# Zero products at five early waits of TensorE, and twelve of its products moved behind the loop

## The chip, the core and the metric

The kernel runs on one core of one Trainium2 chip. The metric is the device time of one execution in microseconds (us). A profile is one execution taken with the hardware profiler; its span runs from the first to the last instruction.

## The reference, cut to what matters

The kernel mixes two branches of the same length (2048 tokens, 512 channels) with a gate per token.

```python
g = sigmoid((x * gate_w).sum(-1, keepdims=True))      # x = A_u, 2048 x 512
# branch a: a long convolution, its taps from 128 complex modes per channel
P = exp(logdA[:, :, None] * l[None, None, :])
K = einsum("dn,dnl,dn->dl", Cc, P, dB).real
y = irfft2(rfft2(pad(u)) * rfft2(pad(K)))[..., :L] + u * Dskip
# branch b: a dense layer, F = 1792
h = gelu(x @ w1 + b1)
b = h @ w2 + b2
return g * a + (1 - g) * b
```

## The kernel before, in words

The program has two parts. `front` computes the dense branch, the taps of the convolution and the first stage of its transforms; `conv` does the second stage, the product of the spectra, the way back and the mixing.

**The dense branch in `front`.** The tokens are cut into eight blocks of 256, and the hidden units into two halves of seven columns of 128, so that the loop `dense` has 16 block steps b (eight blocks with the first half of the units, then the same eight with the second half), each cut into four steps j: step number i = 4b + j, 64 in all. Steps j = 0, 1, 2 hold two columns of hidden units, j = 3 holds one. Every float32 operand is split into a high and a low part of type float32r, so one product becomes three. `hidden(i)` does the products with w1 into a PSUM tile `ph` (lines 901 to 903), ScalarE applies the gelu in place (918) and writes the high part `hh` (921), VectorE writes the low part `hl` (931). `output(i)` multiplies these with w2 into the PSUM tiles `acc` (949 to 951), one for each half (s = 0, 1) of the block's tokens; at j = 3 ScalarE scales the sums with 1 - g (970) and a DMA writes them to the output, the second time with an addition. The tiles `hh` and `hl` are two each and taken in turn. The last block's products with w2 (b = 15, steps 60 to 63) are not done in the loop: `output` puts them on the list `late`.

**The taps and the first stage.** The powers of the modes are built on VectorE and ScalarE, 16 chunks of 2 x 64 small products contract them on TensorE (683), and `first_stage` multiplies with the matrix `c1t` (405): eight short products into four PSUM banks, which ScalarE copies out (423 for the signal, 710 for the taps) to be written to DRAM (`tu_d` at 426, `tk_d` at 725). The signal's copies go through two buffers of the tile `attic`, so that a copy can wait for a DMA of two banks before.

**What sets the order in `front`.** Nothing runs when it is written down. Each piece of work is added to a plan with an engine, a duration, a due time and the tiles it reads and writes; a list scheduler then simulates the engines and emits the pieces in the order that results. An engine's program order is fixed by that, and each engine works its list strictly from the top, with semaphores between engines.

**The end.** `conv` is written in its order by hand: 16 steps s, each with two products of the spectra (1113), the pointwise product on VectorE (1135 to 1140), the way back (`inverse`, 1152), and `turn`: ScalarE copies the result out (1158), SyncE stores it to DRAM (1160), and after each eighth part it is loaded back in another layout (1172), into the tiles `den` and `t3`. The dense branch's sums are loaded to SBUF in pairs of token rows (`dense(k)`, 1186: k of the tuple `HERE` on SyncE's queue during the loop, k of `THERE` on ScalarE's queue behind it). `rest(n)` works off n entries of the list `late`, three products each (1197 to 1199): three entries ahead of the last `inverse`, the others behind the loop. Then come four products (1248) that write a PSUM tile `warm` which nobody reads; then VectorE adds the two late sums to the loaded ones (1251); then 32 products bring the convolution back to tokens (`pb`, 1259), which VectorE (1271) or ScalarE and GpSimd (1268, 1269) scale, add and store (1275, 1273).

Ahead of the first product of `front` stand 13 products of a zero tile `dm` with itself (1010).

Of the kernel before, what the change touches and what calls it, by code (L numbers as in the profile page):

```python
# [9 lines left out]
F32 = mybir.dt.float32  # L10
F32R = mybir.dt.float32r
I32 = mybir.dt.int32
AF = mybir.ActivationFunctionType
ALU = mybir.AluOpType
# [3 lines left out]
P = 128  # L18
L = 2048
D = 512  # L20
# [3 lines left out]
FH = NF // 2  # L24
H = 2
DH = D // H
SB = 256
# [40 lines left out]
D_OUT = -5.37  # L68
N_LATE = 2
N_REST = 3  # L70
N_KEEP = 4

N_ATTIC, N_LOFT, N_TK = 11, 8, 8
ASIDE = (1, 3, 6, 8, 11, 13)
HERE, THERE = (7, 0, 1, 2, 3, 4), (5, 6)
N_DEN = 8
# [200 lines left out]
def gated_mix(  # L277
# [41 lines left out]
    def front(pool, psum, keep, attic, loft, den):  # L319
# [54 lines left out]
        )  # L374
        hh, hl = (tiles(N_HL, [P, 2, SB], n, F32R, keep) for n in ("hh", "hl"))

        io = tiles(2, [P, D], "io")
        gs = pool.tile([P, 16], F32, name="gs")
        dm = pool.tile([P, P], F32, name="dm")
        b2r = pool.tile([P, D], F32R, name="b2r")  # L380
        ones = pool.tile([P, P], F32R, name="ones")
# [11 lines left out]

        def first_stage(xs, due, evac, ahead=2):

            q = (step[0] + ahead) % N_H
            banks = [(phs[q].rearrange("p a b -> p (a b)"), ("h", q)), (pks[0].rearrange("p g s -> p (g s)"), ("pk", 0))]
            banks += [(pus[k], ("pu", k)) for k in range(2)]

            def products():  # L400

                for r, (bank, _) in enumerate(banks):
                    rs = slice(32 * r, 32 * r + 32)
                    for m, (x, _) in enumerate(xs):
                        nc.tensor.matmul(bank[64 * m : 64 * m + 64], c1t[rs], x[rs], start=True, stop=True)  # L405

            mm(1.2, products, due + D_S1, [*(key for _, key in xs), "c1"], [key for _, key in banks], 0.5)
            for r, (bank, key) in enumerate(banks):
                evac(r, bank, key)
# [3 lines left out]
        def signal():  # L413
            for s in range(8):
# [14 lines left out]

                first_stage(xs, t, evac)  # L430
            yield None
# [449 lines left out]
        def halves(i):  # L881

            n = len(cols(i))
            if i in (4 * NB - 4, 4 * NB - 3):
                j = i % 4
                js = slice(2 * j, 2 * j + n)
                return xh[0][:, js], xlo[0][:, js], ("xh", 0, j), ("xl", 0, j)
            k = i % N_HL
            return hh[k][:, 0:n], hl[k][:, 0:n], ("hh", k), ("hl", k)

        def hidden(i, t):
# [4 lines left out]
            def products(n, f):  # L896
                w = f % FH
                for d in range(4):
                    ds = slice(d * P, (d + 1) * P)
# [35 lines left out]
        def output(i, t):  # L935
# [4 lines left out]
            def products(s, a):  # L940
                ss = slice(s * P, (s + 1) * P)
                start = j == 0
                if start and b < NSB:
                    nc.tensor.matmul(a, ones, b2r, start=True, stop=False)
                    start = False
# [9 lines left out]
            for s in range(2):  # L955
                if b == NB - 1 and s >= 2 - N_LATE:
                    for n, f in enumerate(fs):
                        late.append((s, hi[:, n], lo[:, n], wh[1][f % FH], wl[1][f % FH]))
                    continue
# [115 lines left out]
    def conv(pool, ps, late, attic, loft, den):  # L1075
# [112 lines left out]
        def rest(n):  # L1188

            while late and n:  # L1190
# [3 lines left out]
                if first:  # L1194
                    accs[s] = ps.tile([P, D], F32, tag=f"pk{s}", name=f"acc{s}", bufs=1)
                ss = slice(s * P, (s + 1) * P)
                nc.tensor.matmul(accs[s], h[:, ss], w, start=first, stop=False)
# [44 lines left out]
        for k in THERE:  # L1242
            dense(k, nc.scalar)
        rest(14)

        warm = ps.tile([P, D], F32, tag="pa0", name="warm", bufs=1)
        for _ in range(N_KEEP):
            nc.tensor.matmul(warm[0:64], mats[7][1][:, 1], zs[0], start=True, stop=True)
        for s in range(N_LATE):
            z = mos[7][:, s]  # L1250
            nc.vector.scalar_tensor_tensor(z, accs[s], gate[:, 1, 14 + s : 15 + s], z, ALU.mult, ALU.add)

# [103 lines left out]
```

## Time and profile before

| | |
|---|---|
| three timed runs | 532.12, 534.57 and 536.15 us, median 534.57 us |
| the profiled execution | 529.8 us |
| its span | 528.0 us |
| TensorE busy | 509.9 us, 97% of the span |
| VectorE, ScalarE, GpSimd busy | 426.8, 353.5, 41.4 us |
| mean granted TensorE clock | 0.988 |
| DMA | 107.87 MB, mean 204 GB/s |

A busy time counts an instruction from its start to its modelled end; products overlap, so that the distance from start to start is what one costs in a row. "idle before <- releaser" in a row says how long the engine stood still ahead of the instruction, and whose end let it go. PE is TensorE, PEld its loading of weights, DVE VectorE, ACT ScalarE, POOL GpSimd, SP SyncE; a q behind the name is the engine's queue of DMA issues.

### The profile page before, as it was taken

The page shows a single profiled execution, that of the slowest core. Times are in us where ns is not written, and L with a number is a line of the kernel's source. Part 1 is how long each engine was busy: PE and PEld are TensorE (multiplying, and loading weights), DVE is VectorE, ACT ScalarE, POOL GpSimd, SP SyncE. Part 2 cuts the span into 40 slices and gives each one's busy share as a digit, 9 for nine tenths or more (in the row PEclk, how much of TensorE's full clock was granted, in tenths as well). Part 3 has the DMA queues.
Part 4 walks back from the last instruction along what each step waited for, and adds up shares of the span by engine and source line. Part 5 has one row for each costly group of instructions (what it writes and reads, how often), then busy time and mean ns, then how long its engine had stood idle before and what let it go on. Part 6 is the DMA issues. An engine that isn't in the chain of part 4 may idle for free.

```text
span 528.0 us, 12214 instructions
## 1 busy us (share of the span) xinstructions
PE 509.9 (97%) x4818; PEld 386.5 (73%) x4818; DVE 426.8 (81%) x806; ACT 353.5 (67%) x614; POOL 41.4 (8%) x79
## 2 busy tenths in 40 slices
PE   8869999999999999999999999999999999999995
PEld 7537789898889988986998998988889832222441
DVE  5899899999999969879999999999801177777523
ACT  4989946699875599986686998366533545565312
POOL 2000000000000000000112011102010100110113
PEclk9969999999999999999999999999999999999999
DMA  7998674162585434393979027715678988999987
GB/s 248 361 302 300 206 247 137 57 202 61 149 211 216 150 85 129 110 313 84 227 168 269 2 81 134 162 28 121 200 206 171 242 278 303 362 332 397 350 286 287
DMA packets 82517, 107.87 MB, mean 204 GB/s; under 512 B 39334, under 2 KB 43562, under 8 KB 81916
## 3 DMA queue, kind: packets, MB, share of 16 engines
q1 hardware_dynamic: 76476, 85.04, 50.8%
q0 software_dynamic: 5056, 18.65, 13.8%
q10 hardware_dynamic: 928, 3.41, 1.8%
q8 instruction: 38, 0.62, 0.5%
q14 instruction: 19, 0.16, 0.1%
HBM read 61.46 MB, written 45.62 MB: 203 GB/s over the span
## 4 chain that ended last, share of the span: by engine, by line
PE 78%; ACT 10%; DMA 8%; DVE 1%; issue 1%; SPq 1%; ACTq 0%; DVEq 0%
PE pk L683 10%; PE ph L901 8%; PE acc L949 8%; PE ph L903 8%; PE ph L902 8%; PE acc L951 7%; PE acc L950 7%; PE p2u L1113 6%; PE p2k L1113 5%; DMA tu_d<-attic 3%; PE pa L1152 3%; PE pb L1259 3%; PE ph L405 2%; ACT ph L918 2%; ACT L918 1%
## 5 line engine op out<-in xcount | busy, mean ns | idle before, releaser
L901 PE MATMUL ph<-xh,wh 128*128 128x256 f32 x448 | 129.3, 289 | 3.8 <-ACT attic L423 2.2
L903 PE MATMUL ph<-xh,wl 128*128 128x256 f32 x448 | 127.9, 285 | 0.4 <-DVE wl L784 0.2
L902 PE MATMUL ph<-xlo,wh 128*128 128x256 f32 x448 | 127.6, 285 | 0.0
L901 PEld LDWEIGHTS ph<-xh,wh 128*128 128x128 f32 x448 | 86.3, 193 | 14.2 <-issue 5.6
L902 PEld LDWEIGHTS ph<-xlo,wh 128*128 128x128 f32 x448 | 86.4, 193 | 2.0
L903 PEld LDWEIGHTS ph<-xh,wl 128*128 128x128 f32 x448 | 86.2, 192 | 1.0 <-DVE wl L784 1.0
L949 PE MATMUL acc<-wh,hh 128*128 128x512 f32 x210 | 84.6, 403 | 2.4 <-ACT hh L921 2.4
L951 PE MATMUL acc<-wh,hl 128*128 128x512 f32 x210 | 82.5, 393 | 0.0
L950 PE MATMUL acc<-wl,hh 128*128 128x512 f32 x210 | 82.4, 393 | 0.0
L918 ACT ACTIVATE ph<-ph,b1t 128x256 f32<-128x256 f32 x112 | 50.4, 450 | 43.5 <-PE ph L903 41.5
L931 DVE TENSOR_TENSOR hl<-ph,hh 128x512 fp32r<-128x512 f32 (+1 forms) x62 | 38.3, 618 | 30.6 <-ACT hh L921 30.3
L683 PE MATMUL pk<-y,den 128*32 128x64 f32 x2048 | 61.4, 290 | 0.0
L683 PEld LDWEIGHTS pk<-y,den 128*32 128x32 f32 x2048 | 57.2, 136 | 3.7 <-issue 1.4
L949 PEld LDWEIGHTS acc<-wh,hh 128*128 128x128 f32 x210 | 39.5, 188 | 17.1 <-issue 6.8
L951 PEld LDWEIGHTS acc<-wh,hl 128*128 128x128 f32 x210 | 39.4, 188 | 10.0 <-DVE hl L931 1.3
L645 DVE TENSOR_TENSOR y<-y,ea 128x64 f32<-128x64 f32 (+4 forms) x80 | 45.3, 566 | 0.2
L950 PEld LDWEIGHTS acc<-wl,hh 128*128 128x128 f32 x210 | 39.5, 188 | 6.6
L921 ACT CAST hh<-ph 128x512 fp32r<-128x512 f32 (+1 forms) x62 | 33.0, 532 | 10.3 <-PE acc L950 6.9
L490 DVE TENSOR_TENSOR loft<-den,zz 128x256 f32<-128x256 f32 (+2 forms) x48 | 37.3, 776 | 1.8 <-ACT den L616 1.4
L491 DVE TENSOR_TENSOR loft<-den,zz 128x256 f32<-128x256 f32 (+2 forms) x48 | 37.2, 774 | 0.0
L658 DVE TENSOR_TENSOR y<-y,loft 128x2048 f32<-128x2048 f32 x16 | 36.5, 2284 | 0.0
L1121 ACT COPY k<-p2k 128x512 f32<-128x512 f32 x32 | 18.7, 585 | 24.9 <-issue 13.1
(180 smaller groups left out, 876.5 us busy)
## 6 DMA issues: line engine op xcount, KB each, us to landing
tu_d<-attic SPq DMA_DIRECT2D x64, 128.0 KB, 3.4
tk_d<-sk SPq DMA_DIRECT2D x32, 256.0 KB, 5.1
t_d<-sa SPq DMA_DIRECT2D x32, 256.0 KB, 5.5
tk<-tk_d SPq DMA_DIRECT2D x24, 256.0 KB, 3.8
t<-t_d POOLq DMA_DIRECT2D x9, 512.0 KB, 6.9
attic<-in_xt_dram SPq DMA_DIRECT2D x16, 256.0 KB, 4.1
xh_d<-xh SPq DMA_DIRECT2D x8, 512.0 KB, 3.9
xl_d<-xlo SPq DMA_DIRECT2D x8, 512.0 KB, 3.8
```

The costliest lines, as they stand in the source:

```text
L490: vec(2 * m, lambda: vv.tensor_mul(t, a, br), due, [ka, *kb], [kt])
L645: nc.vector.tensor_mul(both(n, 64 - 3 * n, n), both(0, 64 - n, n), an)
L683: nc.tensor.matmul(pks[q][32 * j : 32 * j + 32, :, gg], x[:, r, :, ch], y[:, r, :, ch], start=(r == 0), stop=(r == 1), skip_group_check=True,)
L901: nc.tensor.matmul(p, h, xh[xk][:, d], start=(d == 0), stop=False)
L902: nc.tensor.matmul(p, h, xlo[xk][:, d], start=False, stop=False)
L903: nc.tensor.matmul(p, lo, xh[xk][:, d], start=False, stop=(d == 3))
L918: nc.scalar.activation(phs[q][:, n], phs[q][:, n], AF.Gelu_apprx_tanh, bias=b1t[:, f : f + 1])
L931: nc.vector.tensor_sub(lo, phs[q][:, 0:nf], hi.bitcast(F32))
L949: nc.tensor.matmul(a, h, wh[1][w], start=start, stop=False)
L950: nc.tensor.matmul(a, h, wl[1][w], start=False, stop=False)
L951: nc.tensor.matmul(a, l, wh[1][w], start=False, stop=(j == 3))
L1113: nc.tensor.matmul(out[64 * i : 64 * i + 64], w, x, start=True, stop=True)
```

## The change

Three things change in TensorE's list, and what follows from them elsewhere.

1. A tile `nil` of 128 x 128 zeros is made by GpSimd at the very start, and a helper `busy(n)` multiplies it with itself n times (float32, two passes each). It is called at five places of `front`: 4 times within step 1 ahead of its second column, 5 times ahead of the first output product (step 0), 6 and 4 times in the second `first_stage` of the signal (ahead of its first bank and ahead of its third), and 5 times ahead of step 2's hidden products: 24 products. Where `busy` names no bank, it adds its zeros to the sum in `acc[0]`.
2. The output products of step 58 (b = 14, j = 2: two columns, two token halves, three products each, so twelve) leave the loop and join `late`; they sum up in two more PSUM tiles, in banks `pu2` and `pu3`. For that, `hh` and `hl` get a third tile, which step 58 alone uses. `rest` behind the loop does up to 18 entries where it did up to 14, and VectorE adds four late sums where it added two (0.75 us each in the profile before).
3. The four products into `warm` are gone.

With them the order of the loads changes: the sums of tokens' pair 6 are loaded during the loop (second in `HERE`), and pairs 4 and 5 instead of 5 and 6 behind it. Lines of the changed kernel stand 10 to 16 lower.

```diff
-HERE, THERE = (7, 0, 1, 2, 3, 4), (5, 6)
+HERE, THERE = (7, 6, 0, 1, 2, 3), (4, 5)
-N_LATE = 2
-N_KEEP = 4
+FILL_H, FILL_O, FILL_U = (4, 5), 5, (6, 4)
-        hh, hl = (tiles(N_HL, [P, 2, SB], n, F32R, keep) for n in ("hh", "hl"))
+        hh, hl = (tiles(N_HL + 1, [P, 2, SB], n, F32R, keep) for n in ("hh", "hl"))
+        nil = pool.tile([P, P], F32, name="nil")
+        nc.gpsimd.memset(nil, 0.0)
+
+        def busy(n, bank=None):
+            to = acc[0][:, 0:P] if bank is None else bank[:, 0:P]
+            for _ in range(n):
+                nc.tensor.matmul(to, nil, nil, start=bank is not None, stop=bank is not None)
...
+                busy(fill[0])
                 for r, (bank, _) in enumerate(banks):
+                    if r == 2:
+                        busy(fill[1])
...
-                first_stage(xs, t, evac)
+                first_stage(xs, t, evac, fill=FILL_U if s == 1 else (0, 0))
...
-            k = i % N_HL
+            k = N_HL if i == 4 * NB - 6 else i % N_HL
...
+                if (i, n) == (1, 1):
+                    busy(FILL_H[0], phs[q][:, n])
+                elif (i, n) == (2, 0):
+                    busy(FILL_H[1])
...
+                if (i, s) == (0, 0):
+                    busy(FILL_O, a)
...
-                if b == NB - 1 and s >= 2 - N_LATE:
+                if b == NB - 1 or i == 4 * NB - 6:
                     for n, f in enumerate(fs):
-                        late.append((s, hi[:, n], lo[:, n], wh[1][f % FH], wl[1][f % FH]))
+                        late.append((s + 2 * (NB - 1 - b), hi[:, n], lo[:, n], wh[1][f % FH], wl[1][f % FH]))
...
-                    accs[s] = ps.tile([P, D], F32, tag=f"pk{s}", name=f"acc{s}", bufs=1)
-                ss = slice(s * P, (s + 1) * P)
+                    accs[s] = ps.tile([P, D], F32, tag=f"pu{s}" if s > 1 else f"pk{s}", name=f"acc{s}", bufs=1)
+                ss = slice(s % 2 * P, s % 2 * P + P)
...
-        rest(14)
-
-        warm = ps.tile([P, D], F32, tag="pa0", name="warm", bufs=1)
-        for _ in range(N_KEEP):
-            nc.tensor.matmul(warm[0:64], mats[7][1][:, 1], zs[0], start=True, stop=True)
-        for s in range(N_LATE):
-            z = mos[7][:, s]
-            nc.vector.scalar_tensor_tensor(z, accs[s], gate[:, 1, 14 + s : 15 + s], z, ALU.mult, ALU.add)
+        rest(18)
+
+        for s in range(4):
+            m, i = 7 - s // 2, s % 2
+            z, g = mos[m][:, i], gate[:, 1, 2 * m + i : 2 * m + i + 1]
+            nc.vector.scalar_tensor_tensor(z, accs[s], g, z, ALU.mult, ALU.add)
```

TensorE's order near the end of the loop, before: the last six of step 58's twelve output products (those into `acc1` with `hh0`), the six of step 59 (`hh1`), and the first hidden products of step 61.

```order
L950 MATMUL acc1_86<-wl14_135,hh0_138 128x512
L951 MATMUL acc1_86<-wh14_121,hl0_140 128x512
L949 MATMUL acc1_86<-wh15_122,hh0_138 128x512
L950 MATMUL acc1_86<-wl15_136,hh0_138 128x512
L951 MATMUL acc1_86<-wh15_122,hl0_140 128x512
L949 MATMUL acc0_85<-wh16_123,hh1_139 128x512
L950 MATMUL acc0_85<-wl16_137,hh1_139 128x512
L951 MATMUL acc0_85<-wh16_123,hl1_141 128x512
L949 MATMUL acc1_86<-wh16_123,hh1_139 128x512
L950 MATMUL acc1_86<-wl16_137,hh1_139 128x512
L951 MATMUL acc1_86<-wh16_123,hl1_141 128x512
L901 MATMUL ph1_88<-xh10_107,wh02_112 128x256
```

The same place in the changed kernel, from the last hidden product of step 60 on.

```order
L917 MATMUL ph0_87<-xh10_107,wl01_125 128x256
L965 MATMUL acc0_85<-wh16_123,hh1_139 128x512
L966 MATMUL acc0_85<-wl16_137,hh1_139 128x512
L967 MATMUL acc0_85<-wh16_123,hl1_142 128x512
L965 MATMUL acc1_86<-wh16_123,hh1_139 128x512
L966 MATMUL acc1_86<-wl16_137,hh1_139 128x512
L967 MATMUL acc1_86<-wh16_123,hl1_142 128x512
L915 MATMUL ph1_88<-xh10_107,wh02_112 128x256
```

All twelve products of step 58 are gone from here; step 59's now follow step 60's hidden products directly. Nothing else in the order of this place has moved.

They stand again behind the loop, as `acc2` and `acc3` with the third tile `hh2`; here the last of the six rows with `acc2`, the six with `acc3` and the first of the final products `pb`, in the changed kernel.

```order
L1215 MATMUL acc2_5517<-wh15_122,hl2_143 128x512
L1213 MATMUL acc3_5524<-wh14_121,hh2_140 128x512
L1214 MATMUL acc3_5524<-wl14_135,hh2_140 128x512
L1215 MATMUL acc3_5524<-wh14_121,hl2_143 128x512
L1213 MATMUL acc3_5524<-wh15_122,hh2_140 128x512
L1214 MATMUL acc3_5524<-wl15_136,hh2_140 128x512
L1215 MATMUL acc3_5524<-wh15_122,hl2_143 128x512
L1273 MATMUL pb00_5535<-den_78,g1t_4807 64x512 x2
L1273 MATMUL pb01_5536<-den_78,g1t_4807 64x512 x2
```

The twelve products have taken the place of the four into `warm`, which stood directly ahead of `pb00`.

The third place is early in TensorE's list: the second first stage of the signal and the start of step 2, in the changed kernel, with the semaphores that each row waits for.

```order
L386 MATMUL acc_85<-nil 128x128 x6
L415 MATMUL ph_89<-attic,c1t 64x512 [waits DMAHW2_49,Activation_49]
L415 MATMUL ph_89<-ux_103,c1t 64x512 [waits DMAHW3_49]
L415 MATMUL pk_90<-attic,c1t 64x512 [waits Activation_49]
L415 MATMUL pk_90<-ux_103,c1t 64x512
L386 MATMUL acc_85<-nil 128x128 x4
L415 MATMUL pu_91<-attic,c1t 64x512 [waits Activation_49]
L415 MATMUL pu_91<-ux_103,c1t 64x512
L415 MATMUL pu_92<-attic,c1t 64x512 [waits Activation_49]
L415 MATMUL pu_92<-ux_103,c1t 64x512
L386 MATMUL acc_85<-nil 128x128 x5
L915 MATMUL ph_89<-xh_106,wh_114 128x256 [waits Activation_49]
```

The three rows with `nil` are added; they wait for nothing, and each stands directly ahead of a row that waits. The rows around them are those of before, in the same order. ScalarE's list is the same as before throughout, and the planner's order of all other work too.

2 lines of the change are left out of this document (1 added, 1 removed).

## The prediction

> **What bounds the kernel now.** I read the page's first part and its shares of the chain of work that ended last.
>
> ```profile
> PE 509.9 (97%) x4818; PEld 386.5 (73%) x4818; DVE 426.8 (81%) x806; ACT 353.5 (67%) x614; POOL 41.4 (8%) x79
> PE 78%; ACT 10%; DMA 8%; DVE 1%; issue 1%; SPq 1%; ACTq 0%; DVEq 0%
> ```
>
> TensorE (PE) is busy for 97% of the span and makes 78% of the chain. The 8% of DMA must lie somewhere too. Busy time by stage, with instruction counts and the granted clock, separates the stages:
>
> ```profile
> 26.40:30.00 3.60, 1.56 (x6) 0.53 (x4) 3.42 (x12) 3.58 (x8) 0.00 (x0) 1.00 0.91 260
> 30.00:33.00 3.00, 1.80 (x13) 0.51 (x14) 2.96 (x8) 2.99 (x5) 0.00 (x0) 0.63 0.97 278
> 36.00:39.60 3.60, 3.54 (x16) 3.55 (x17) 3.60 (x6) 2.16 (x4) 0.00 (x0) 0.50 1.05 376
> 39.60:43.00 3.40, 3.40 (x26) 1.96 (x24) 2.98 (x8) 3.34 (x7) 0.00 (x0) 0.80 0.78 221
> 60.00:100.00 40.00, 40.00 (x474) 33.85 (x473) 39.28 (x73) 26.53 (x46) 0.25 (x2) 1.00 0.46 152
> 240.00:395.00 155.00, 155.00 (x1862) 135.59 (x1860) 138.25 (x247) 103.00 (x169) 17.71 (x31) 1.00 0.55 139
> 460.00:490.00 30.00, 30.00 (x157) 8.18 (x152) 24.34 (x40) 16.61 (x32) 3.75 (x8) 1.00 1.00 367
> ```
>
> The columns are the stretch, its length, then PE, PEld, DVE, ACT, POOL, the clock, the DMA share and GB/s. From 60 us on PE hardly rests: a product removed there is time gained. Before, it rests, and from about 31 to 41 us it has lost its clock: 0.63, 0.50, 0.80 in the three stretches. Whether that costs anything depends on who is late there, which the chain in order of time tells:
>
> ```profile
> 33.65 0.45 SPq L426
> 34.16 3.68 DMA tu_d<-attic
> 37.91 0.59 ACT attic L423
> 48.32 5.01 DMA tu_d<-attic
> 57.48 0.60 ACT io L970
> 58.13 0.50 PE acc L944
> ```
>
> The chain runs through the signal's stores to `tu_d`, the copies on ScalarE that wait for their two buffers (423), ScalarE's other work, and reaches PE only at 58.13. PE's own waits in this stretch are in its timeline:
>
> ```profile
> 13.49 0.39 PE L901 MATMUL ph<-xh,wh 128*128 128x256 f32 x1 [1.59 <-DVE wh L780]
> 17.87 0.50 PE L949 MATMUL acc<-wh,hh 128*128 128x512 f32 x1 [1.97 <-ACT hh L921]
> 29.26 1.04 PE L405 MATMUL ph<-attic,c1t 32*64 32x512 f32 x2 [2.04 <-DMA attic<-in_xl_dram]
> 32.56 1.11 PE L405 MATMUL pu<-attic,c1t 32*64 32x512 f32 x1 [1.20 <-ACT attic L423]
> 36.05 0.58 PE L901 MATMUL ph<-xh,wh 128*128 128x256 f32 x1 [1.52 <-ACT attic L423]
> 47.10 0.39 PE L901 MATMUL ph<-xh,wh 128*128 128x256 f32 x1 [0.72 <-ACT attic L423]
> 58.13 0.50 PE L944 MATMUL acc<-b2r,ones 128*128 128x512 f32 x1 [0.90 <-ACT io L970]
> ```
>
> The first five are the five places of the change. The last two matter most: after the cold stretch PE still arrives early, twice, and stands for ScalarE.
>
> **Part 1: the zero products.** They add 24 products of 128 columns in two passes. The nearest row is that of the products ahead of the first step, 26 passes of the same shape:
>
> ```profile
> 1.00 5.92 PE L1010 MATMUL pk<-dm 128*128 128x128 f32 x26 [1.00 <-POOL dm L1005]
> 0.74 0.20 POOL L1005 MEMSET dm<- 128x128 f32 x1 [0.29 <-POOLq L1337]
> ```
>
> 5.92 / 13 = 0.455 us a product is the upper end. The lower end takes a quarter of the 0.43 us that a pass of 512 columns into `warm` costs (shown below): 0.107 a pass, 0.215 a product. So the five fills cost 0.86 to 1.82, 1.08 to 2.28, 1.29 to 2.73, 0.86 to 1.82 and 1.08 to 2.28 us against waits of 1.59, 1.97, 2.04, 1.20 and 1.52. At the lower end all lie inside their waits. At the upper end they overrun by 0.23 + 0.31 + 0.69 + 0.62 + 0.76 = 2.61 us, of which the waits at 47.10 and 58.13 take 0.72 + 0.90 = 1.62, so that about 1.0 us would reach the path. I take zero: the clock was full ahead of the first three fills. Behind the fills stand, on PE's list, first-stage products that ScalarE copies out, and step 2's hidden products, whose gelu ScalarE only reaches behind its own queue, so a small overrun makes nobody late.
>
> What can the fills win? If they hold the clock, step 2's 24 hidden products, which begin at 36.05, run faster. The stretch from 36 to 39.6 has 17 of their weight loads in 3.60 us, 0.21 each; at full clock it is
>
> ```profile
> 45.86 0.28 PE L901 MATMUL ph<-xh,wh 128*128 128x256 f32 x1
> 45.98 0.28 PE L902 MATMUL ph<-xlo,wh 128*128 128x256 f32 x1
> ```
>
> 0.12 from start to start: 24 x 0.09 = 2.2 us. But what follows is the row at 47.10, where PE already waits 0.72 us for a copy on ScalarE, and ScalarE hangs on the DMAs of the chain, not on PE. The 2.2 us turn into a longer wait at 47.10 and at 58.13. I take zero of it, and keep 2.2 as the other end.
>
> The new `memset` on GpSimd comes ahead of the `memset` of `dm` and shifts GpSimd's start by its 0.20 us. PE's first products follow, but the wait of 1.59 at 13.49 swallows that; of SyncE's first loads some may shift by up to 0.2 us. I take 0.1.
>
> **Part 2: twelve products leave the loop.** The first and the thirteenth of the last 18 output products in the loop:
>
> ```profile
> 409.13 0.39 PE L949 MATMUL acc<-wh,hh 128*128 128x512 f32 x1
> 411.88 0.39 PE L949 MATMUL acc<-wh,hh 128*128 128x512 f32 x1
> ```
>
> The twelve before the thirteenth are step 58's: 411.88 - 409.13 = 2.75 us. PE is full there, so whatever follows comes 2.75 us sooner, provided its inputs do. Step 59's six products need `hh` and `hl` of their step, ready long enough by VectorE's row:
>
> ```profile
> 405.99 0.42 DVE L931 TENSOR_TENSOR hl<-ph,hh 128x256 fp32r<-128x256 f32 x1 [2.62 <-ACT hh L921]
> ```
>
> It ends at 406.41, against 409.13. Between loop and second stage, PE waits for the last gelu and a copy, both behind PE's own last hidden product, so they shift along.
>
> **Part 3: behind the loop.** Here the twelve products add 2.75 us again, and `warm` goes:
>
> ```profile
> 505.11 3.15 PE warm L1248 x7
> 508.69 13.77 PE pb L1259 x61
> 505.52 0.14 PEld L1248 LDWEIGHTS warm<-z,cc 128*64 128x64 f32 x1 [0.29 <-issue]
> 507.67 0.14 PEld L1248 LDWEIGHTS warm<-z,cc 128*64 128x64 f32 x1 [0.29 <-issue]
> ```
>
> `warm` is four products of two passes; their weight loads, the second and the seventh shown, follow each other at (507.67 - 505.52) / 5 = 0.43 us, so eight passes hold PE for 3.44 us. The chain goes from `rest` through it into `pb` without a gap. If `pb` may start as soon as `rest` ends, the end moves by -2.75 + 2.75 - 3.44 = **-3.44 us**. What would be late next are the DMAs that `pb` reads, which have so far been hidden behind `rest` and `warm`. Their issues, the time to landing of the first of each, and PE's first use of `t3`:
>
> ```profile
> 502.75 1.16 ACTq L1172 DMA_DIRECT2D den<-t_d  x2
> 504.01 1.84 ACTq L1172 DMA_DIRECT2D t<-t_d  x3
> den<-t_d ACTq DMA_DIRECT2D x1, 256.0 KB, 3.0
> t<-t_d ACTq DMA_DIRECT2D x1, 512.0 KB, 5.8
> 511.11 0.19 PEld L1259 LDWEIGHTS pb<-t,g1t 128*64 128x64 f32 x2
> ```
>
> `den` lands at 502.75 + 3.0 = 505.75 and the first of `t3` at 504.01 + 5.8 = 509.81. Both follow the last `inverse`, so they move to 503.0 and 507.06. PE then wants `den` at about 505.1 and `t3` at 511.11 - 3.44 = 507.67: margins of 2.1 and 0.6 us. The second is thin, and the DMAs are full in the second stage (a share of 1.00 in 460 to 490), so they may not come the whole 2.75 us sooner. If they came no sooner at all, `t3` would hold `pb` to 509.81, which is 1.30 us sooner than the 511.11 of before instead of 3.44. I take 0.1 us for this, with both ends kept.
>
> VectorE's two further additions take 0.75 us each; the last starts when `rest` ends and is over at about 505.9, ahead of the first `pb` sum, which comes at 509.60 - 3.44 = 506.16 by this row:
>
> ```profile
> 509.60 0.75 DVE L1271 SCALAR_TENSOR_TENSOR attic<-pb,gate,attic 128x512 f32<-128x512 f32 x1 [3.70 <-PE pb L1259]
> ```
>
> The bank of `acc3` is wanted by the fourth `pb` sum, later still. The token pair 6, which these additions need, is loaded during the loop, tens of us ahead.
>
> **The sum.** 0 (fills) + 0.1 (start) - 2.75 + 2.75 - 3.44 + 0.1 (landing) = -3.24, so about 3.2 us off: the profiled execution would go from 529.8 to 526.6 us. The three runs lie 2.3 to 6.4 us above the profiled one; taking the same off their median gives 534.57 - 3.2 = **531.4 us**, 0.6% less. A measurement of this kernel can tell about 1% from no change.
>
> **The rivals.**
> *The DMAs hold the end.* They stay where they are, the gain is the 1.30 us above: 533.3 us. For it speaks the full share, against it that from 423 to 429 us the share is far lower, so there is room to start sooner.
>
> ```profile
> 427.00:429.00 2.00, 2.00 (x12) 0.68 (x10) 2.00 (x4) 1.40 (x3) 0.00 (x0) 1.00 0.49 119
> ```
>
> *The early clock is worth its time.* In executions without the profiler, PE may be colder for longer and reach 58 us last; then the fills save the 2.2 us above: 534.57 - 3.2 - 2.2 = 529.2. The spread of the three runs, 4 us, allows it; the waits at 47.10 and 58.13 speak against it.
>
> *Slower: the end runs at half clock.* Without `warm`, PE may stand ahead of `pb` or of `t3`. The early stretch shows what follows from thin work: after waits of 2.04 and 1.20 us with first-stage products between, the clock went to 0.50, for about 10 us (31 to 41). If the same befell `pb`, its products, one pair of passes in 0.43 us, would take double: 10 us at half pace lose 5 us, with the wait of 2 us that starts it 7; against 3.44 gained that is 3.6 slower: 538.1 us. It decides from a wait of some 2 us on, that is if the DMAs land 1.4 us or more later than the margin allows. The Trainium skill, "TensorE: Matmul & The Clock Gate", section "HAM oscillation — how this bites in real kernels", gives as the rule that only idle gaps of PE above about 3.4 us bring the clock down; by it a wait of 2 us would cost nothing but itself, and the time would be 531.4 + 2 = 533.4. The trace does not bear it out: no gap from 26.4 to 36.05 us exceeds 2.04, and the clock still halved; so this rival keeps a small chance.
>
> *The change doesn't do what it says:* the fills start too late or run half-clocked, and their 1.0 us comes on top: 531.4 + 1.0 = 532.4, inside my range.
>
> **How the numbers follow.** Forecast 55% (alone 530.0 to 533.0), DMAs 15%, early clock 17%, half clock at the end 7%, the rest 6%, spread (fills that cost are among it). The range takes in the first three with the runs' own spread around them: 526.5 to 535.5 us. Faster by over 1% means below 529.2: about half of the early-clock case and some luck of the runs, 0.18. Slower by over 1% means above 539.9: the worse part of the half-clock case and the unexplained, 0.08. Within 1%: 0.74.
>
> **What would show it.** In the changed profile: zero products inside all five early waits, a clock of 1.00 in 30 to 41 us, and longer waits at the two rows now at 47.10 and 58.13, the latter's start unmoved; the second stage 2.75 us sooner; `pb` directly behind `rest`, at about 505, with at most 0.5 us of waiting for `t3`. Wrong would be a start at 58 that moved by over 1 us, a wait of PE in the second stage, or a clock below 1.00 at the end.

## The result, and the profile after

In the session with the first measurement the changed kernel took 528.67 us (median of six runs, 526.88 to 530.85) against 535.21 us for the kernel before (six runs, 531.36 to 536.15). The ratio is 0.990, with a 95% interval of 0.9862 to 0.9938: 5.3 us less, between 3.3 and 7.4. (It is not the quotient of the two medians, which lie 6.5 us apart.) Measured again in a later session it was 0.9916 (0.9884 to 0.9948), 4.5 us less. The forecast was 531.4 us, 3.2 us less, inside 526.5 to 535.5.

The profiled execution took 528.3 us with a span of 526.5 (before 529.8 and 528.0). The first part of the page after, and its shares of the chain:

```profile
PE 509.1 (97%) x4858; PEld 387.8 (74%) x4858; DVE 428.4 (81%) x808; ACT 353.0 (67%) x614; POOL 41.6 (8%) x80
PE 75%; ACT 11%; DMA 8%; DVE 3%; issue 2%; SPq 1%; ACTq 0%; DVEq 0%
```

Forty more instructions on TensorE and about the same busy time: 48 zero passes came, eight warming ones went. Busy time by stage, with the granted clock as the third number from the end, in the stretches that were cold before:

```profile
30.00:33.00 3.00, 3.00 (x20) 1.35 (x16) 2.76 (x9) 2.99 (x5) 0.00 (x0) 1.00 0.91 232
36.00:39.60 3.60, 3.49 (x30) 3.19 (x36) 3.60 (x4) 1.91 (x4) 0.00 (x0) 1.00 0.98 340
39.60:43.00 3.40, 1.45 (x14) 0.30 (x14) 2.33 (x7) 3.34 (x7) 0.00 (x0) 1.00 0.59 157
43.00:46.00 3.00, 3.00 (x24) 2.45 (x21) 2.46 (x10) 2.93 (x5) 0.00 (x0) 1.00 1.04 351
```

The clock is full throughout (0.63, 0.50 and 0.80 before). TensorE's timeline shows the five fills and the waits of TensorE from there to 60 us:

```profile
12.12 1.05 PE L386 MATMUL ph<-nil 128*128 128x128 f32 x8
15.19 1.28 PE L386 MATMUL acc<-nil 128*128 128x128 f32 x10
17.91 0.50 PE L965 MATMUL acc<-wh,hh 128*128 128x512 f32 x1 [1.21 <-ACT hh L935]
26.77 1.50 PE L386 MATMUL acc<-nil 128*128 128x128 f32 x12
28.91 1.04 PE L415 MATMUL ph<-attic,c1t 32*64 32x512 f32 x2 [0.64 <-DMA attic<-in_xl_dram]
30.49 1.16 PE L386 MATMUL acc<-nil 128*128 128x128 f32 x8
33.62 1.38 PE L386 MATMUL acc<-nil 128*128 128x128 f32 x10
36.11 0.39 PE L915 MATMUL ph<-xh,wh 128*128 128x256 f32 x1 [1.11 <-ACT attic L433]
42.55 0.64 PE L415 MATMUL pu<-attic,c1t 32*64 32x512 f32 x1 [1.95 <-ACT attic L433]
47.41 0.38 PE L915 MATMUL ph<-xh,wh 128*128 128x256 f32 x1 [0.72 <-ACT attic L433]
58.32 0.50 PE L960 MATMUL acc<-b2r,ones 128*128 128x512 f32 x1 [0.79 <-ACT io L986]
```

A fill of 12 passes takes 1.50 us, 0.125 a pass. Behind three of the fills a wait is left (1.21, 0.64 and 1.11 us); the products behind the first and the fourth, at 13.16 and 31.58 us, wait no longer and start sooner than before (13.49 and 32.56). What TensorE gained between 36 and 43 us it hands back in a new wait of 1.95 us at 42.55, and it starts at 58.32, where it started at 58.13. The end of the chain:

```profile
495.77 0.60 ACT sa L1174
...
496.51 6.42 DMA t_d<-sa
...
503.02 2.87 DMA den<-t_d
...
506.02 13.97 PE pb L1273 x64
...
520.02 0.75 DVE attic L1285
```

`pb` begins 2.67 us sooner than before (508.69), and in this execution it waits for `den`: the last store to `t_d` took 6.42 us. VectorE's last operation ends 2.46 us sooner. The end of the span moved by only 1.5 us because what follows that operation took 5.7 us (526.5 - 520.77) instead of 4.8 (528.0 - 523.23); in the other profiles below it takes 4.7 to 7.4, whatever the kernel.

### The profile page after: what moved, and what is told of

It reads as the page before. It is cut to its first block, busy times and chain, and to the rows that moved or that the text cites. A ratio compares the mean times of both kernels' runs of the same rounds, so it can differ in the third digit from the quotient of the medians.

```text
span 526.5 us, 12296 instructions
## 1 busy us (share of the span) xinstructions
PE 509.1 (97%) x4858; PEld 387.8 (74%) x4858; DVE 428.4 (81%) x808; ACT 353.0 (67%) x614; POOL 41.6 (8%) x80
## 4 chain that ended last, share of the span: by engine, by line
PE 75%; ACT 11%; DMA 8%; DVE 3%; issue 2%; SPq 1%; ACTq 0%; DVEq 0%
PE pk L693 10%; PE ph L915 8%; PE ph L917 8%; PE ph L916 8%; PE acc L965 8%; PE acc L967 7%; PE acc L966 7%; PE p2u L1129 6%; PE p2k L1129 5%; PE pa L1168 3%; PE pb L1273 3%; DMA tu_d<-attic 2%; PE ph L415 2%; ACT L932 2%; ACT ph L932 2%
## 5 line engine op out<-in xcount | busy, mean ns | idle before, releaser
L915 PEld LDWEIGHTS ph<-xh,wh 128*128 128x128 f32 x448 | 85.1, 190 | 11.9 <-issue 5.6
L916 PEld LDWEIGHTS ph<-xlo,wh 128*128 128x128 f32 x448 | 85.2, 190 | 2.0
L917 PEld LDWEIGHTS ph<-xh,wl 128*128 128x128 f32 x448 | 85.1, 190 | 1.2 <-DVE wl L794 1.2
L965 PE MATMUL acc<-wh,hh 128*128 128x512 f32 x206 | 82.9, 403 | 1.3 <-ACT hh L935 1.2
L967 PE MATMUL acc<-wh,hl 128*128 128x512 f32 x206 | 81.1, 394 | 0.4 <-DVE hl L945 0.4
L966 PE MATMUL acc<-wl,hh 128*128 128x512 f32 x206 | 80.9, 393 | 0.0
```

Of the source, the lines that this page charges most:

```text
L915: nc.tensor.matmul(p, h, xh[xk][:, d], start=(d == 0), stop=False)
L916: nc.tensor.matmul(p, h, xlo[xk][:, d], start=False, stop=False)
L917: nc.tensor.matmul(p, lo, xh[xk][:, d], start=False, stop=(d == 3))
L965: nc.tensor.matmul(a, h, wh[1][w], start=start, stop=False)
L966: nc.tensor.matmul(a, h, wl[1][w], start=False, stop=False)
L967: nc.tensor.matmul(a, l, wh[1][w], start=False, stop=(j == 3))
```

## The experiments

All ratios are against runs of the kernel before in the same session; the sessions of the experiments ran on three different chips. This table has from each profile the starts, in us, of the first tap product (683 before, 693 after), of the second stage (1113, 1129), and of `pb`, with TensorE's wait for `den` ahead of it.

| kernel | first tap product | second stage | `pb` | wait |
|---|---|---|---|---|
| before | 65.97 | 420.53 | 508.69 | 0 |
| changed | 66.18 | 418.29 | 506.02 | 0.42 |
| fills alone | 67.56 | 422.75 | 510.92 | 0 |
| move alone | 67.23 | 419.93 | 507.25 | 0 |
| no `warm` | 67.49 | 423.03 | 509.37 | 1.74 |
| changed with `warm` | 67.92 | 421.31 | 512.21 | 0 |
| more fills | 65.87 | 420.62 | 507.94 | 0 |
| double fills | 66.47 | 420.37 | 507.68 | 0 |
| changed again | 66.92 | 419.02 | 506.33 | 0 |
| stores split | 67.97 | 420.32 | 507.62 | 0 |
| stores split, more fills | 66.16 | 419.85 | 507.15 | 0 |
| more fills again | 67.13 | 420.64 | 509.06 | 1.11 |
| eight elsewhere | 66.15 | 418.63 | 505.94 | 0 |
| third stage and sixteen | 67.90 | 420.62 | 507.93 | 0 |

Two things are to be read from it first. The first column differs by 1.5 us between kernels with the same program up to that point (before and no `warm`), and by 1.7 among the changed kernel, its repeat and the one with `warm`: a single profile cannot size the fills. And from the second stage to `pb` it is 87.30 to 87.32 us in every kernel with the move and without `warm` in which `den` was in time, against 88.16 before: that part is TensorE's program alone.

### The two halves of the change

The fills alone: the kernel before with the 24 zero products; the twelve products stay in the loop and `warm` stays behind it.

```diff
+        nil = pool.tile([P, P], F32, name="nil")
+        nc.gpsimd.memset(nil, 0.0)
...
+                busy(fill[0])
...
+                if (i, s) == (0, 0):
+                    busy(FILL_O, a)
```

> The kernel before plus the 24 zero products and nothing else. Theory A (the early stretch hangs on ScalarE and the DMAs, PE only waits): clock 1.00 in 30 to 41 us, the start at 58 us unmoved, time within 1 us of before. Theory B (in the timed runs PE is colder than in the profiled one and is late at 58 us): the mean clock of the runs goes from about 0.98 to 0.99 or more, and the median falls by 3 to 5 us, most of the change's 6.5.

532.12 us, ratio 0.9981 (0.9962 to 1.0): 1.0 us less, between 2.0 and nothing. Busy time and clock by stage in the profile of this kernel:

```profile
43.00:46.00 3.00, 2.46 (x6) 0.85 (x7) 2.46 (x10) 2.95 (x4) 0.00 (x0) 0.50 1.08 367
46.00:49.00 3.00, 3.00 (x16) 3.00 (x15) 3.00 (x6) 2.92 (x7) 0.00 (x0) 0.50 0.94 305
```

The row of TensorE's timeline that begins the cold stretch:

```profile
43.54 1.11 PE L415 MATMUL pu<-attic,c1t 32*64 32x512 f32 x1 [1.94 <-ACT attic L433]
```

The cold spell has not gone but moved: the wait that the faster TensorE now has in the third first stage of the signal, 1.94 us with thin products around it, takes the clock to 0.50 from 43 to 49 us. In the profile of the changed kernel the same wait (1.95 us) did not. The time fell as the first theory allows (1 us at most); 3 to 5 us, as the second has it, lie outside the interval, though the mean clock of the runs did rise, from 0.985 to 0.99 in the median.

In its new place the cold spell is not free. The chain of work that ended last, in this profile:

```profile
43.00 0.50 ACT attic L433
43.54 1.97 PE pu L415 x4
45.51 0.51 PE ph L915
```

From 43.54 on the chain stays on TensorE up to the first tap product: TensorE waits for ScalarE neither near 47 nor near 58 us, since it now comes too late there itself. From the product at 43.54 to the first tap product it is 24.02 us here. Five profiles of this study have a wait at the same product and a full clock behind it (changed, move alone, no `warm`, stores split with more fills, third stage and sixteen): there it is 23.0 to 23.6 us, of which 0.9 to 1.5 are waits and 22.1 are work. So the cold clock cost TensorE 1.9 us, of which the waits took up the larger part and 0.4 to 1.0 us were paid.

The move alone: the changed kernel with all fills at nothing and without `nil`.

```diff
-FILL_H, FILL_O, FILL_U = (4, 5), 5, (6, 4)
+FILL_H, FILL_O, FILL_U = (0, 0), 0, (0, 0)
...
-        nil = pool.tile([P, P], F32, name="nil")
-        nc.gpsimd.memset(nil, 0.0)
+        nil = None
```

> The changed kernel without its zero products. Theory A: 3.2 us faster than before if TensorE sets the end, 1.3 to 1.5 us if the DMAs behind the last store to t_d hold it. Theory B: the same 1.3 to 1.5 us; the mean clock of the runs stays at the level of before.

528.52 us, ratio 0.9929 (0.9897 to 0.996): 3.8 us less, between 2.1 and 5.5. The clock is at half early on, as before (0.50 from 33 to 39.6 us), and the end of the chain has no wait:

```profile
507.02 0.23 PE acc L1214
507.25 13.91 PE pb L1272 x64
521.18 0.75 DVE attic L1284
```

What the move is worth can be read more closely than from the times. The start of the last chunk of tap products, of the second stage, and of VectorE's last operation, in the kernel before:

```profile
382.82 3.84 PE L683 MATMUL pk<-y,den 128*32 128x64 f32 x128
420.53 1.08 PE L1113 MATMUL p2k<-tk,cc 128*64 128x512 f32 x4
522.48 0.75 DVE attic L1271
```

The first two in this kernel; the third stands in the chain above:

```profile
384.95 3.84 PE L692 MATMUL pk<-y,den 128*32 128x64 f32 x128
419.93 1.08 PE L1128 MATMUL p2k<-tk,cc 128*64 128x512 f32 x4
```

From the last chunk to the second stage it is 37.71 us before and 34.98 here: 2.73 less. From there to VectorE's last operation it is 101.95 and 101.25: 0.70 less. Both repeat within 0.02 us in the other profiles, the first in all kernels with the move (34.98 or 34.99) and all without (37.70 or 37.71), the second wherever the loads at the end were in time.

So the move is worth what the sum gave it, and the fills about 1 us more. The two ratios multiply to 0.991, which is the whole change.

### What `warm` hid

The kernel before without `warm`, the twelve products still in the loop:

```diff
-        warm = ps.tile([P, D], F32, tag="pa0", name="warm", bufs=1)
-        for _ in range(N_KEEP):
-            nc.tensor.matmul(warm[0:64], mats[7][1][:, 1], zs[0], start=True, stop=True)
```

> The kernel before without the four products into warm, whose result nobody reads. If TensorE sets the end: 3.4 us faster, pb at 505.2. If the DMAs hold it: den lands at about 505.8, so pb waits 0.6 us or so for it and the end comes 1.5 to 2.5 us sooner; the moved products would then add little. If the wait costs the clock: pb at half clock, 3 to 6 us slower.

532.08 us, ratio 0.9975 (0.9948 to 1.0003): 1.3 us less, where the products that went had held TensorE for 3.44. TensorE's timeline tells where the rest is:

```profile
509.37 3.65 PE L1256 MATMUL pb<-den,g1t 128*64 128x512 f32 x16 [1.74 <-DMA den<-t_d]
```

And the busy time by stage, with the clock, around and behind this wait:

```profile
508.00:510.00 2.00, 0.63 (x4) 0.40 (x6) 0.42 (x1) 0.00 (x0) 0.00 (x0) 1.00 0.89 307
510.00:515.00 5.00, 4.85 (x25) 1.69 (x22) 2.21 (x3) 1.38 (x2) 2.38 (x2) 1.00 0.92 347
```

Without the twelve products behind the loop, `rest` ends before `den` is there. `warm` covered that landing; in the changed kernel the moved products do. Behind this wait comes a shorter one for the first load of `t3` (`t` in the rows), which the chain goes through:

```profile
507.51 5.52 DMA t<-t_d
513.17 10.54 PE pb L1256 x48
```

The stretch from the second stage to VectorE's last operation is 100.70 us here, 1.25 shorter than before (101.95): of the 3.44, 1.74 went in the wait for `den` and 0.45 in the one for `t3`. That agrees with the 1.3 us of the timed runs. And after 1.74 us of standing still the clock stayed at 1.00.

The changed kernel with the four products of `warm` put back behind `rest`:

```diff
         rest(18)
+        warm = ps.tile([P, D], F32, tag="pa0", name="warm", bufs=1)
+        for _ in range(4):
+            nc.tensor.matmul(warm[0:64], mats[7][1][:, 1], zs[0], start=True, stop=True)
```

> The changed kernel with the four products into warm put back behind the late products. TensorE then starts pb as late as before (about 508.5 us). If TensorE sets the end, this costs the 3.4 us again and leaves only what the zero products bring; if the DMAs hold the end, it costs less than 3.4, 1 to 2 us. Against before: Theory A 0 to 1 us faster, Theory B 3 to 5 us faster.

531.2 us, ratio 0.9965 (0.9942 to 0.9988), 1.9 us less than before and so 2.6 more than the changed kernel's 0.9916. In the chain they stand where they stood:

```profile
508.63 3.15 PE warm L1264 x7
511.84 0.37 PE warm L1264
512.21 13.76 PE pb L1277 x61
```

From 508.63 to 512.21 it is 3.58 us. With the move done TensorE pays for all of `warm`: from the second stage to VectorE's last operation it is 104.69 us, 3.44 more than the 101.25 without it. The difference of the ratios, 2.6 us, is between two sessions and has an uncertainty of some 2; 1.9 us less than before lies between what the two theories gave.

### Filling the moved cold spell

Three and five zero products more, in the third first stage of the signal:

```diff
+                    if r == 3 and len(fill) > 2:
+                        busy(fill[2])
...
-                first_stage(xs, t, evac, fill=FILL_U if s == 1 else (0, 0))
+                first_stage(xs, t, evac, fill=FILL_U if s == 1 else (3, 0, 5) if s == 2 else (0, 0))
```

> The changed kernel plus eight zero products in the signal's third first stage: three ahead of its first bank and five ahead of its fourth, where two profiles with zero products showed a wait of TensorE of up to 1.95 us at 42 us and, behind it, half clock from 43 to 52 us. Theory C (the zero products move the cold spell from 31 to 41 us, where it is free, to 43 to 52 us, where part of it is paid): clock 1.00 throughout, mean clock of the runs 0.996 or more with little spread, and 1 to 2 us faster than the changed kernel run beside it. Theory A alone (the early stretch hangs on ScalarE and the DMAs): no difference.

530.3 us, ratio 0.9947 (0.9917 to 0.9976). The clock of this kernel is now full everywhere, 0.997 in the median of its runs, against 0.992 for the changed kernel and 0.984 for the kernel before. By slices of the span:

```profile
PEclk9999999999999999999999999999999999999998
```

Its two further fills in TensorE's timeline:

```profile
38.81 0.83 PE L386 MATMUL acc<-nil 128*128 128x128 f32 x6
41.17 1.38 PE L386 MATMUL acc<-nil 128*128 128x128 f32 x10
```

Yet it is no faster than the changed kernel; it tends to be slower, and the gain of 1 to 2 us that theory C gave did not come. It does not follow that a cold clock at 43 to 52 us is free: the loss stands elsewhere. By the table the stretch from the first tap product to the second stage is 354.75 us (420.62 - 65.87), in the changed kernel 352.11, and that hides what a clock kept full before 66 us may have brought. The profiles show this to be small. In five of the kernels with zero products (fills alone, changed with `warm`, double fills, stores split, eight elsewhere) the clock is below 1.00 behind 43 us and the chain runs over TensorE from there to the first tap product, without the waits near 47 and 58 us; from the product that began it to there, 22.8 to 24.4 us pass, where 23.0 to 23.6 pass with a full clock. So what was paid lies between nothing and some 1.4 us.

All fills doubled, 48 products in the first five places:

```diff
-FILL_H, FILL_O, FILL_U = (4, 5), 5, (6, 4)
+FILL_H, FILL_O, FILL_U = (8, 10), 10, (12, 8)
```

> The changed kernel with twice the zero products at each of the five places, 48 instead of 24: 6 us more work for TensorE, of which some 4.4 us lie beyond the waits they stand in (at 0.125 us a pass). Theory A: the waits that follow (1.95, 0.72 and 0.79 us at 42, 47 and 58 us in the profile of the changed kernel) swallow 3.5 us of it, and the time rises by 1 us or less. If TensorE set the early stretch: 4 to 6 us slower than the changed kernel.

529.17 us, ratio 0.9927 (0.9895 to 0.9959). 11.7 us of zero products instead of 6.4 do not show in the time beyond the uncertainty of 1.7 us. Two of the fills and the wait behind them:

```profile
26.84 2.84 PE L386 MATMUL acc<-nil 128*128 128x128 f32 x24
33.71 2.50 PE L386 MATMUL acc<-nil 128*128 128x128 f32 x20
43.65 0.64 PE L415 MATMUL pu<-attic,c1t 32*64 32x512 f32 x1 [1.97 <-ACT attic L433]
```

They overrun the first five waits, and TensorE still stands 1.97 us at 43.65: it has time to spare up to here. Behind it the clock is at 0.75 and 0.68 (43 to 46 and 46 to 49 us) and no wait follows up to the first tap product.

The changed kernel once more, unedited, beside these two:

> The changed kernel as it is, beside the others of this study on one chip. From the parts (zero products alone 0.9981, moved products alone 0.9929): 0.991 of before if they add up, mean clock about 0.992.

528.48 us, ratio 0.9916 (0.9884 to 0.9948). Its profile has the cold spell that the first one lacked (0.66 and 0.77):

```profile
43.00:46.00 3.00, 2.68 (x10) 1.54 (x11) 2.46 (x10) 2.95 (x4) 0.00 (x0) 0.66 1.01 304
46.00:49.00 3.00, 3.00 (x22) 3.00 (x22) 3.00 (x7) 2.84 (x7) 0.00 (x0) 0.77 0.91 314
```

One program, two executions, cold in one and not in the other, and `pb` directly behind `rest` here where the first profile waits 0.42 us.

### Where more fills lose: ScalarE's copy at 265 us?

In the profile of more fills ScalarE waits 7.10 us at 265.81 for a store to `tu_d`, and TensorE behind it 0.8 us at 269; before, ScalarE's wait there was 4.73 us. Half of those stores (those of the signal's last first stage) were moved from SyncE's to GpSimd's queue; the order of the other engines stays as it was.

```diff
-                            128, lambda m=m: nc.sync.dma_start(rows[:, 8 * s + 4 * m + r], st[k][64 * m : 64 * m + 64]),
+                            128, lambda m=m: (nc.gpsimd if s == 7 and m else nc.sync).dma_start(rows[:, 8 * s + 4 * m + r], st[k][64 * m : 64 * m + 64]),
```

In the changed kernel:

> The changed kernel, but the second halves of the signal's last eight stores to tu_d (at about 255 to 268 us) are issued by GpSimd instead of SyncE. Theory D (early gains are given back at ScalarE's copy that waits there for SyncE's queue of stores): the copy at about 264 us comes 2 us or more sooner; TensorE waited there 0 to 0.4 us in the changed kernel, so the time falls by 0 to 0.5 us only: ratio to before 0.989 to 0.992. Theory E (VectorE's chain of powers sets the stretch from 120 to 290 us, whatever the stores do): the copy comes sooner and the time stays, ratio 0.990 to 0.993. The changed kernel alone does not tell the two apart; the next kernel does.

528.56 us, ratio 0.9918 (0.9891 to 0.9944). The same edit in the kernel with more fills:

> The kernel with eight more zero products in the third first stage, and the same stores moved to GpSimd's queue. Theory D: TensorE's wait of 0.8 us for the high part at about 269 us is gone, the stretch from the first tap product to the second stage is 1 to 1.6 us shorter than with more fills alone (354.75 us), and the time is 1 to 1.6 us below that kernel. Theory E: the wait moves to a VectorE product within 30 us, the stretch stays at 354 to 355 us, and the time agrees with that of more fills alone within 0.5 us.

528.53 us, ratio 0.9935 (0.991 to 0.9961). And that kernel without the edit again:

> The kernel with eight more zero products once more, beside the two others. Theory D and E: TensorE waits 0.5 to 2 us at about 269 us behind ScalarE's copy, the stretch is 354 to 355.5 us, ratio to before 0.992 to 0.997. If the long waits of the single profiles were chance, the stretch is 352 to 353 us here and the ratio 0.989 to 0.992.

530.26 us, ratio 0.9969 (0.9945 to 0.9993). The copy on ScalarE in these three, in the same order:

```profile
265.52 0.59 ACT L433 COPY attic<-pu 128x512 f32<-128x512 f32 x1 [6.83 <-DMA tu_d<-attic]
```

```profile
265.03 0.59 ACT L435 COPY attic<-pu 128x512 f32<-128x512 f32 x1 [5.98 <-DMA tu_d<-attic]
```

```profile
265.84 0.58 ACT L435 COPY attic<-pu 128x512 f32<-128x512 f32 x1 [5.80 <-DMA tu_d<-attic]
```

The copy did not come 2 us sooner with half of the queue gone, and in the third kernel TensorE does not wait at 269 at all. The edit did not shorten what it was to shorten, so neither theory was put to its test; as the explanation of the loss the copy falls, since the loss is there without TensorE's wait. The kernel with more fills and the split stores came out 1.8 us faster than without the split, with intervals that overlap. That more fills cost time is likely but not firm: 0.9969 stands beside 0.9918 in one session, 2.7 us apart, with intervals that just miss each other, but the 0.9918 is that of the changed kernel with the split stores; with the split in both it is 0.9935 beside 0.9918, within the uncertainty. The unedited changed kernel was not run beside these three.

What the three profiles with eight more fills share lies earlier, on VectorE. Its row for the load of `pr`, first in more fills, then in more fills again, then in the changed kernel's repeat:

```profile
130.20 0.69 DVE L532 TENSOR_TENSOR pr<-pr,dtb 128x512 f32<-128x512 f32 x1 [1.76 <-DMA pr<-in_prm_dram]
```

```profile
131.37 0.69 DVE L532 TENSOR_TENSOR pr<-pr,dtb 128x512 f32<-128x512 f32 x1 [1.71 <-DMA pr<-in_prm_dram]
```

```profile
129.69 0.69 DVE L530 TENSOR_TENSOR pr<-pr,dtb 128x512 f32<-128x512 f32 x1 [0.21 <-DMA pr<-in_prm_dram]
```

The load is issued at 126.17 us in the second and at 125.98 in the third: it takes 5.2 us there and 3.7 here. VectorE is 1.5 us later for it, and the first stage of the taps, which TensorE begins at 131 to 133 us, takes 1.86 to 2.01 us in the three profiles instead of 1.04: 0.8 to 1.0 us of standing.

### Is it the number of instructions?

The zero products lengthen TensorE's program. The profile's page lists two queues of kind instruction (38 and 19 packets in the changed kernel), so the supposition was that what is loaded of the program during the run falls elsewhere in time; no run here shows it. Two kernels separate the number of products from their place. Eight more products, none of them in the third first stage (32 in all):

```diff
-FILL_H, FILL_O, FILL_U = (4, 5), 5, (6, 4)
+FILL_H, FILL_O, FILL_U = (4, 9), 9, (6, 4)
```

> The changed kernel with eight more zero products, as many as in the kernel with more fills, but at the first output product and step 2's hidden products (32 in all), none in the third first stage. Theory F (where TensorE's program stands, not what is filled, makes VectorE's load of pr late: eight more instructions on TensorE's list move its code loads): VectorE waits 1.5 to 1.8 us for pr at about 130 us, VectorE's two long products before and after it stand 20.2 to 20.4 us apart, TensorE waits 0.6 to 0.8 us at 132, the cold spell at 43 to 52 us stays, ratio to before 0.993 to 0.997. Theory G (the fills in the third first stage do it, through the times they shift): wait for pr 0.2 to 0.4 us, distance 18.6 to 19.2 us, ratio 0.989 to 0.993.

530.22 us, ratio 0.9964 (0.9939 to 0.9989). And the eight in the third first stage with sixteen more in the first five places (48 in all):

```diff
-FILL_H, FILL_O, FILL_U = (4, 5), 5, (6, 4)
+FILL_H, FILL_O, FILL_U = (6, 10), 10, (8, 6)
```

> The kernel with more fills (eight in the third first stage) and sixteen further zero products spread over the first five places, 48 in all, as many as in the doubled kernel. Theory F: as in the doubled kernel VectorE waits 0.2 to 0.4 us for pr at about 130 us, distance of its long products 18.6 to 19.2 us; clock 0.99 to 1.00 throughout; the stretch from the first tap product to the second stage is 352 to 353 us and the ratio to before 0.987 to 0.992. Theory G: wait 1.5 to 1.8 us, distance 20.2 to 20.4 us, stretch 353.5 to 354.8 us, ratio 0.993 to 0.997.

529.87 us, ratio 0.9948 (0.9927 to 0.9968). VectorE's row in these two:

```profile
129.86 0.69 DVE L530 TENSOR_TENSOR pr<-pr,dtb 128x512 f32<-128x512 f32 x1 [1.16 <-DMA pr<-in_prm_dram]
```

```profile
131.28 0.69 DVE L532 TENSOR_TENSOR pr<-pr,dtb 128x512 f32<-128x512 f32 x1 [0.83 <-DMA pr<-in_prm_dram]
```

1.16 and 0.83 us lie between what the two theories gave. The ratio of the first is where theory F had it, that of the second where theory G had it. Eight products seem to cost time without standing in the third first stage, which speaks against the place; 48 with eight of them there seem to cost some as well, which speaks against the number alone. Both are measured against the changed kernel's 0.9916 of another session and chip, with intervals that overlap its own. In the first of the two the profiled execution had the shortest span of all, 526.0 us, although its timed runs are slow. Neither theory is shown, and why the kernels with eight more fills came out 1 to 3 us slower, and the doubled one within the uncertainty, **stays open**. No kernel with more fills than 24 had a lower ratio than the changed kernel.

## Why the prediction was right, and where it was off

**The sum.** Of the -3.24 us the move and the end of `warm` were -3.44 and two corrections of 0.1. The move alone measured -3.8 (-2.1 to -5.5). In the profiles the loop gives 37.71 - 34.98 = 2.73 us behind the last chunk of tap products, where the sum had 2.75, and the part from the second stage to VectorE's last operation 101.95 - 101.25 = 0.70, where 3.44 - 2.75 is 0.69. The two together are 3.43. This part of the sum was right in its mechanism and to 0.01 us in its size, wherever the loads at the end came in time.

**The fills.** The term was 0, with bounds of -2.2 and +1.0; measured -1.0 (0 to -2.0). That is the step that was mis-sized. Its reasoning held in the profile of the changed kernel: no fill made a product late, the clock is full from 30 to 41 us, the start at 58 moved by 0.2 us. The sentence that failed is "The 2.2 us turn into a longer wait at 47.10 and at 58.13": these two did not grow (0.72 and 0.79 us, before 0.72 and 0.90). The wait came earlier, 1.95 us at 42.55, a place that the prediction had not named, and in other executions it brings a cold spell of its own, behind which TensorE is late for ScalarE instead of waiting for it. About half of what the rival *the early clock is worth its time* asked for (2.2 us) was there; its interval includes nothing at all. How a full clock there saves the 1 us was not found: the stretches of single profiles vary by more, and in the three profiles without zero products (before, move alone, no `warm`) TensorE waits for ScalarE at 58 to 60 us in spite of the early cold clock. The rival is not out, though. Among the 95 timed runs of the kernel before in the four later sessions, the colder ones were the longer ones: the correlation within the sessions is -0.43, and 0.01 less of mean clock goes with 2.2 us more. That is what an early clock worth some of its time would look like, but a correlation does not show which is the cause. The first session's 5.3 us exceeds 3.24 + 1.0 by 1.1, inside its own interval; the repeat's 4.5 exceeds it by 0.3.

**The DMAs at the end.** The margin of 2.1 us for `den` was reckoned from a landing that comes 2.75 us sooner. It did not hold in every execution: in the first profile the store to `t_d` ahead of it took 6.42 us, the whole margin went, and 0.42 us of waiting came. The margin was taken from the best case: the load of `den` is issued 82.22 us behind the start of the second stage in the profile before and 82.4 to 85.4 us behind it in the thirteen others, and lands some 3.0 us later, where `pb` wants it after 87.3. In ten profiles with the move and without `warm`, two wait for `den` (0.42 and 1.11 us), eight do not. So the rival *the DMAs hold the end* is a case of some executions. With `warm` gone and nothing moved its one profile shows 1.74 us; an estimate makes it the rule there, since `pb` would want `den` after 84.6 us and even the earliest issue plus 3.0 us gives 85.2. `t3`, held to be the thinner margin at 0.6 us, kept `pb` waiting by 0.45 us there and hardly elsewhere.

**The half clock at the end** did not come. The longest wait ahead of `pb`, 1.74 us, left the clock at 1.00; the 2 us from which this rival was to decide were not reached, so that it is untested there. The Trainium skill, "TensorE: Matmul & The Clock Gate", section "HAM oscillation — how this bites in real kernels", names idle gaps above about 3.4 us as what brings the clock down. The end of the kernel agrees with it. The early stretch does not: after 1.94 us, with thin products on both sides, the clock was at 0.50.

**Slower** had its chance of 0.08; no run came near it. The second stage was to begin 2.75 us sooner and began 2.24 sooner in the first profile, of which the later start takes 0.21 and the loop's 2.73 instead of 2.75 another 0.02; the other 0.28 were lost between the first tap product and the last chunk (66 to 383 us), where the programs are the same.

One detail of the text above: the copies of the signal go through three buffers of `attic`, not two, so a copy can wait for a DMA of three banks before. No number hangs on it.

## What to carry to other kernels

An instruction that fills a gap at the end may be the cover of a transfer: taken out alone it gave back 1.3 of its 3.44 us, and only with useful work moved into the same place the whole. A cold clock in a stretch where another engine is late costs only what exceeds the waits that follow, and curing it moves the wait on, here by 6 us, instead of removing it; so look for the next wait before pricing the gain. When times are too noisy for a term of the sum, look for a stretch that TensorE works through without waiting: here such stretches repeated to 0.02 us, while the times of one kernel lay several us apart. More of a cure that worked is a new kernel to be measured: with eight further zero products the ratio was 0.2 to 0.5% higher, though in the third first stage they gave a full clock.

## What the runs showed that was not expected

A wait of 1.9 to 2.0 us between products of 32 rows brought TensorE's clock to between 0.50 and 0.77 in several profiles and left it at 1.00 in another with the same program; a wait of 1.74 us behind dense products left it at 1.00.

Between executions of the same program up to there the first tap product starts 1.5 to 1.7 us apart, and what follows the last operation takes 4.7 to 7.4 us. Two profiles therefore can't price an effect of 1 us by their spans, though 87.31 us from the second stage to `pb` repeats to 0.02.

From kernel to kernel the time did not follow the clock: the highest mean clock (0.997 to 0.998, with more fills) went with ratios of 0.9935 to 0.9969, the changed kernel's 0.992 with 0.9916.

The same load of `pr`, issued at nearly the same time, took 3.7 us in the changed kernel's repeat and 5.1 to 5.3 in the three profiles of kernels with eight more products of zeros, in the third first stage, on an engine that has nothing to do with it (4.3 with sixteen further ones).
